# Linear attention with a gated feed-forward block on one core: the last rows' stacks spread over two stages, the bias loaded into the accumulators

## The chip, the cores and the metric

The kernel runs on one core of a Trainium2 chip. The metric is the device time of one execution in microseconds; lower is better. The core's engines work side by side, each through its own list of instructions: TensorE (PE) multiplies matrices, VectorE (DVE), ScalarE (ACT) and GpSimd (POOL) work on tiles, and the Sync queue (SP) issues most of the transfers (DMAs). A core has 16 DMA engines for them.

## The reference

With x of 2048 rows by 576 columns, 32 heads of 18 columns and a hidden width of 4608:

```
xn = layernorm(x)
q, k, v = split(xn @ wqkv)                       # per head
phi(t) = where(t > 0, t + 1, exp(t)) + 1e-6
kv = sum_s phi(k)[s] v[s]^T ; z = sum_s phi(k)[s]
o  = (phi(q) kv) / (phi(q) z + 1e-6)
s  = o @ wo
g  = silu(gelu(xn @ w1 + b1) @ w2 + b2)
out = x + s * g
```

All is float32. The matrix products are made from operands split into a high and a low part (hi: a rounded copy; lo: the difference), three products of parts for one.

## The kernel before

**Three stages.** The kernel is one long list, written out by hand. Every product runs on TensorE; around it a table `plans` holds what the other engines do and after which step of TensorE's work it is issued (`add(step, function)` puts an entry, `at_step(step)` issues the entries of a step in the order in which they were put). `in_order` makes the order of the list binding on each engine.

*Keys and values* (pairs p = 0 to 7, steps p * 14 + k, lines 542 to 775): a pair is two tiles of 128 rows of x. They are loaded, normalized, transposed and split; stored for later (`x_store`); a projection `Proj` (line 362) makes the keys of both tiles from seven products in the order 1, 6, 7, 5, 2, 4, 3, then `Plain` makes the values, and `do_state` (step 3) adds the pair before to the state. Beside it, operands for the second feed-forward matrix are prepared: `w2_sum` adds blocks, `w2_hi` (line 530) copies the hi part on ScalarE, `w2_lo` subtracts on VectorE and stores the result to memory. `W2_SPLITS` says at which (pair, step of hi, step of lo).

*Queries* (iterations r = 0 to 9, steps (8 + r) * 14 + k, lines 793 to 1218): `Proj` again makes queries of two tiles, phi and the denominators follow on ScalarE, VectorE and GpSimd, `transpose_p` transposes the quotients, and `Attend` of two iterations before multiplies them by the state folded with wo.

*Feed-forward* (two halves of x's rows with nine chunks of hidden columns each, 28 steps a chunk, lines 1613 to 1728): `Up` makes hidden columns with seven products (steps 0 to 13), gelu and the hi/lo split `HOps` follow, and `product` multiplies by W2 into four accumulators C11, C12, C21, C22 and a helper U1 of the tile `macc` (steps 14 to 27). At a chunk's steps 12, 13, 15 and 17 of a half's first chunk `set_bias` (line 1257) fills the accumulators with b2. Later chunks' weight operands are loaded on the Sync queue at given steps (`W1Loaded` makes its tiles and loads; `W2_NEXT` for W2).

**The wait that the restart of bank e can bring.** A projection has four accumulators in PSUM: a, b, z, e. Product 5 goes into e, VectorE adds it to a running term (line 399, through the helper at line 386), and product 3, the last, goes on adding into the same bank:

```
elif i == 5:
    self.mm(E, 5, (1, 1))
    add1(b[:, HD:], E, self.u2)
...
elif i == 3:
    self.mm(E, 3, (1, 2), first=False)
    add1(a[:, HD:], E, self.u1)
```

**The stacks of the last rows.** 576 rows are four tiles of 128 and 64 rows left over. For these `Rest` (line 912) makes stacks, seven in all: two of x's, five of W1's. A stack is loaded (256 KB); `hi(g)` and `lo(g)` split three (g = 0) or four (g = 1) of its column blocks on ScalarE and VectorE; `sums` makes on VectorE, between the two groups, four sums in place that group 1 is made of; `store(g)` writes hi and lo, each twice, to memory from where the feed-forward stage loads them. The load lies in iteration r = 1 to 6 (stack 0 before the iterations) at step 1; hi, lo of group 0 and the sums at step 2 of the next iteration (step 5 for r = 1), group 1 three steps later, stores two steps after each.

**Pools.** The groups' tiles come from `w1r`, tag `stw`, two buffers that are taken in turn. The same tag serves the operands of `w2_hi`, the temporaries of `wkq.sums` and the raw W1 tiles. The stack's raw columns come from `stage`, six buffers, as the x tiles do.

**The bias.** `load_bias` (line 1250) loads b2, the same row in all 128 partitions, into a tile with the tag `w2t6`, which is also the tag of `load_sum(7)` (line 1331), issued at step 5 of chunks 0 to 7. It runs before the first chunk and at step 2 of the second half's first chunk. `set_bias` copies from the tile.

## Time and profile before

| | |
|---|---|
| median of three runs | 1129.63 us (1128.88 to 1129.68) |
| the profiled execution | 1128.63 us, span 1126.9 us |
| granted TensorE clock, mean | 0.993 |
| busy: PE, PE weight loads | 97%, 90% |
| busy: DVE, ACT, POOL | 73%, 46%, 40% |
| moved by the DMA engines | 295.02 MB, mean 262 GB/s |

A page of the profile gives busy times and the chain of work that ended last; the other views answer for a stretch, a line or a tile. In a row of the waits stand engine, tile and line of the instruction that waited, what released it, and total, number and longest of the waits in us. In a timeline row stand start, duration, engine, line, operation, what is written from what, and in square brackets the idle time ahead of it with the releaser. A row of the windows has the busy time of PE, weight loads, DVE, ACT and POOL in a stretch with the number of instructions, then the granted clock (1.00 is full), the mean share in which the DMA engines were busy, and GB/s. Where TensorE's clock is granted at less than 1.00, part of the stretch ran slower. Pairs 2 to 6 of the first stage begin at 48.9, 65.85, 83.08, 100.31 and 117.55 us, the queries at about 150 us, the feed-forward stage at about 308 us and its second half at about 713 us.

### The profile page before, as it was taken

How to read it: one execution, taken by the hardware profiler on the slowest of the kernel's cores; microseconds unless marked ns; L12 is line 12 of the kernel's file. 1: busy time of each engine (PE TensorE's matmuls, PEld its weight loads, DVE VectorE, ACT ScalarE, POOL GpSimd, SP SyncE). 2: the span in 40 equal slices, each digit the busy share in tenths (PEclk: the TensorE clock that was granted, in tenths of full speed). 3: DMA queues.
4: the chain of work that ended last, by engine and by line, in shares of the span. 5: the costliest groups of instructions: out<-in, count | busy, mean ns of one | idle time of the engine just before them, and what ended most of it. 6: DMA issues, size and time to landing. Idle time of an engine off the chain costs nothing.

```text
span 1126.9 us, 18961 instructions
## 1 busy us (share of the span) xinstructions
PE 1096.0 (97%) x6888; PEld 1011.6 (90%) x6888; DVE 822.2 (73%) x1288; ACT 517.4 (46%) x945; POOL 456.0 (40%) x417
## 2 busy tenths in 40 slices
PE   8999997898999999999999999999999999999998
PEld 8999997888989989889899899898998998989988
DVE  6777577778578878888888888675575664765866
ACT  7776454454564543544545435444233242332342
POOL 6853522454552644534525434224133232241310
PEclk9999998999999999999999999999999999999999
DMA  5997839898998796886977969998767667767243
GB/s 199 320 287 263 287 90 316 303 358 301 318 380 271 269 359 202 294 314 220 341 249 248 360 170 351 381 356 305 221 221 226 211 222 229 222 221 236 86 151 116
DMA packets 115771, 295.02 MB, mean 262 GB/s; under 512 B 12189, under 2 KB 31133, under 8 KB 113631
## 3 DMA queue, kind: packets, MB, share of 16 engines
q1 hardware_dynamic: 110207, 282.61, 71.2%
q0 software_dynamic: 4896, 10.03, 5.3%
q8 instruction: 54, 0.88, 0.3%
q10 hardware_dynamic: 576, 1.18, 0.3%
q14 instruction: 38, 0.31, 0.1%
HBM read 180.39 MB, written 108.66 MB: 256 GB/s over the span
## 4 chain that ended last, share of the span: by engine, by line
PE 69%; DMA 1%; DVE 1%; ACT 1%; issue 1%; DVEq 0%; ACTq 0%
PE pm L1418 34%; PE zy L1279 10%; PE a L1279 10%; PE e L1279 10%; PE b L1279 5%; PE pd L1533 2%; DMA op<-w 1%; DMA op_b<-wb 1%; DVE macc L1526 0%; ACT macc L1527 0%; DVE h_l L1000 0%; DVE b L1305 0%; ACT g L1287 0%; ACT L1287 0%; DVE xs L1477 0%
## 5 line engine op out<-in xcount | busy, mean ns | idle before, releaser
L997 ACT CAST h_h<-g 128x512 fp32r<-128x512 f32 x204 | 120.1, 621 | 135.9 <-PE pm L1418 134.9
L1000 DVE TENSOR_TENSOR h_l<-g,h_h 128x512 fp32r<-128x512 f32 x204 | 160.2, 785 | 3.8 <-ACT h_h L997 3.8
L1426 DVE TENSOR_TENSOR macc<-macc,pm 128x576 f32<-128x576 f32 x136 | 102.1, 751 | 39.3 <-PE pm L1418 39.3
L1279 PE MATMUL a<-xH,wa 128*128 128x512 f32 x288 | 101.4, 393 | 0.0
L1428 DVE TENSOR_TENSOR macc<-pm,macc 128x576 f32<-128x576 f32 x98 | 74.2, 757 | 21.9 <-PE pm L1418 20.2
L1386 POOL TENSOR_TENSOR mid<-g 128x512 f32<-128x512 f32 x34 | 45.4, 1334 | 100.2 <-ACT g L1287 100.2
L1287 ACT ACTIVATE g<-b,b1c 128x512 f32<-128x512 f32 x36 | 24.8, 688 | 131.7 <-DVE b L1305 131.7
L1296 ACT COPY mid<-a 128x512 f32<-128x512 f32 x36 | 21.2, 588 | 94.1 <-PE a L1279 94.1
L1279 PEld LDWEIGHTS a<-xH,wa 128*128 128x128 f32 x288 | 54.0, 188 | 11.3
L1380 POOL TENSOR_TENSOR g<-g 128x512 f32<-128x512 f32 x34 | 50.6, 1490 | 24.1 <-DVE h_l L1000 22.5
L1299 DVE TENSOR_TENSOR mid<-b,mid 128x512 f32<-128x512 f32 x36 | 24.7, 685 | 44.6 <-PE b L1279 42.7
L1279 PE MATMUL a<-xL,wa 128*128 128x512 f32 x144 | 56.2, 390 | 0.0
L1383 POOL TENSOR_TENSOR g<-g 128x512 f32<-128x512 f32 x34 | 50.8, 1493 | 11.3 <-DVE h_l L1000 9.0
L1504 POOL TENSOR_TENSOR fin1l<-fin1h,fin1l 128x288 f32<-128x288 f32 x8 | 6.5, 807 | 120.5 <-PE pm L1418 44.5
L1279 PE MATMUL e<-xSH,wb 128*128 128x512 f32 x144 | 50.4, 391 | 0.8 <-DVE b L1305 0.8
L1279 PE MATMUL zy<-xSH,w 128*128 128x512 f32 x144 | 50.9, 394 | 0.0
L1279 PE MATMUL zy<-xH,w 128*128 128x512 f32 x144 | 50.8, 394 | 0.0
L1279 PE MATMUL b<-xSH,w 128*128 128x512 f32 x144 | 50.5, 391 | 0.0
L1279 PE MATMUL e<-xSH,w 128*128 128x512 f32 x144 | 50.4, 390 | 0.0
L1024 POOL TENSOR_TENSOR mid<-w1raw 128x256 f32<-128x256 f32 x17 | 14.9, 877 | 85.4 <-DMA w1raw<-w 51.0
L1377 POOL TENSOR_TENSOR g<-g 128x512 f32<-128x512 f32 x34 | 47.6, 1399 | 2.7
L1000 DVE TENSOR_TENSOR h_l<-mid,h_h 128x512 fp32r<-128x512 f32 x34 | 42.3, 1245 | 7.3 <-ACT h_h L997 7.3
(965 smaller groups left out, 3674.0 us busy)
## 6 DMA issues: line engine op xcount, KB each, us to landing
op<-w SPq DMA_DIRECT2D x72, 256.0 KB, 5.3
w<-op SPq DMA_DIRECT2D x72, 256.0 KB, 3.6
we<-we_dram SPq DMA_DIRECT2D x36, 448.0 KB, 4.8
w2raw<-w SPq DMA_DIRECT2D x10, 1152.0 KB, 10.1
op<-w2o SPq DMA_DIRECT2D x19, 576.0 KB, 6.1
w1raw<-w SPq DMA_DIRECT2D x18, 512.0 KB, 6.4
op_a<-wa SPq DMA_DIRECT2D x18, 512.0 KB, 4.5
wa<-op_a SPq DMA_DIRECT2D x18, 512.0 KB, 4.3
```

The costliest lines, as they stand in the source:

```text
L997: nc.scalar.copy(pair[0], src)
L1000: eng.tensor_tensor(pair[1], src, pair[0].bitcast(F32), op=SUB)
L1279: nc.tensor.matmul(ps.rearrange("p (c j) -> p c j", c=4), st, mv, start=first and n == 0, stop=n == len(seq) - 1, skip_group_check=True,)
L1287: nc.scalar.activation(g, ps, AF.Gelu_apprx_tanh, bias=b1c[:, f : f + 1])
L1299: tt(u1_sb, B, m1_sb, op=ADD)
L1377: tt(src[5, pr], A(1, 1), A(1, 0), op=SUB)
L1380: tt(src[6, pr], src[5, pr], A(0, 0), op=ADD)
L1383: tt(src[3, pr], src[6, pr], A(0, 1), op=SUB)
L1386: tt(src[7, pr], A(0, 0), A(1, 0), op=SUB)
L1418: nc.tensor.matmul(ps[:, q, :HD], hs[p][st][:, cs], m[:, p, :], start=(n == 0 and i not in CHAIN), stop=(n == len(seq) - 1), skip_group_ch ...
L1426: nc.vector.tensor_tensor(dst, dst, src, op=SUB)
L1428: nc.vector.tensor_tensor(dst, src, dst, op=ADD)
```

## The change

`Rest` moves ahead of the first stage, keeps a tile for each group, and its `sums` takes the engine as an argument. A table places all seven stacks: three (x's first, W1's first and second) beside keys and values, the other four in the queries, mostly one group an iteration. An entry gives the load as (pair or iteration + 8, step), the step of group 0's lo, place and engine of the sums, and the step of group 1's lo; hi comes one step before lo, the store one step after (two in one case).

```
+    REST_PLAN = {
+        (0, True): ((2, 12), (3, 2), (3, 4, GP), (4, 2)),
+        (0, False): ((4, 0), (5, 2), (5, 13, DV), (6, 2)),
+        (1, False): ((4, 7), (5, 2), (5, 13, DV), (6, 2)),
+        (2, False): ((8, 9), (9, 12), (9, 12, DV), (10, 6)),
+        (3, False): ((9, 9), (10, 6), (10, 11, DV), (11, 6)),
+        (4, False): ((11, 1), (12, 6), (12, 9, DV), (13, 6)),
+        (1, True): ((13, 1), (14, 6), (14, 9, DV), (15, 6)),
+    }
+
+    def plan_rests():
+        for key, (load, first, (p, k, eng), second) in REST_PLAN.items():
+            add(load[0] * NSP + load[1], lambda key=key: rests.update({key: Rest(*key)}))
+            for g, (q, at) in enumerate((first, second)):
+                step = q * NSP + at
+                add(step - 1, lambda key=key, g=g: rests[key].hi(g))
+                add(step, lambda key=key, g=g: rests[key].lo(g))
+                add(step + (2 if step == 9 * NSP + 12 else 1), lambda key=key, g=g: rests[key].store(g))
+            add(p * NSP + k, lambda key=key, eng=eng: rests[key].sums(eng))
+
+    plan_rests()
     for p in range(1, NPAIR):
         plan_pair(p)
...
-    rests = {0: Rest(0, True)}
-    RESTS = ((0, True), (0, False), (1, False), (2, False), (3, False), (4, False), (1, True))
...
-        if 0 < r < NPAIR - 1:
-            i, of_x = RESTS[r]
-            add(base + 1, lambda r=r, i=i, of_x=of_x: rests.update({r: Rest(i, of_x)}))
-        if 1 <= r < NPAIR:
-            at = base + (5 if r == 1 else 2)
-            for g, k in ((0, 0), (1, 3)):
-                add(at + k, lambda r=r, g=g: rests[r - 1].hi(g))
-                add(at + k, lambda r=r, g=g: rests[r - 1].lo(g))
-                add(at + k + 2, lambda r=r, g=g: rests[r - 1].store(g))
-            add(at, lambda r=r: rests[r - 1].sums())
```

One split of a W2 operand moves from steps 4 and 6 of pair 5 to steps 7 and 9:

```
-        (2, 4, 6), (2, 9, 12), (3, 4, 6), (3, 9, 12), (4, 4, 6), (4, 9, 12), (5, 4, 6), (6, 7, 9), (7, 1, 3),
+        (2, 4, 6), (2, 9, 12), (3, 4, 6), (3, 9, 12), (4, 4, 6), (4, 9, 12), (5, 7, 9), (6, 7, 9), (7, 1, 3),
```

The bias is loaded straight into the first of four row blocks of C11 and of C22, and `set_bias` copies from there to the other three blocks and to C21 and C12. In the second half the load moves from step 2 to step 8, behind the W2 load that stands at that step; two loads of W2 operands come eight steps earlier:

```
+    BIAS = (C11, C22)
+
     def load_bias():
-        b2b = fr.tile([P, 2, HD], F32, tag="w2t6", name="b2b", bufs=1)
-        nc.sync.dma_start(
-            b2b.rearrange("p a b -> p (a b)"), bass.AP(tensor=b2.tensor, offset=b2.offset, ap=[[0, P], [1, D]])
-        )
-        tails["b2"] = b2b
+        for h, m in enumerate(BIAS):
+            src = bass.AP(tensor=b2.tensor, offset=b2.offset + h * HD, ap=[[0, P], [1, HD]])
+            nc.sync.dma_start(macc[:, 0, m, :], src)
 
     def set_bias(s):
-        h = int(s in (C12, C22))
-        nc.scalar.copy(macc[:, :, s, :], tails["b2"][:, h : h + 1].to_broadcast([P, QH, HD]))
+        m = BIAS[s in (C12, C22)]
+        at = slice(s == m, QH)
+        dst = macc[:, at, s, :]
+        nc.scalar.copy(dst, macc[:, 0:1, m, :].to_broadcast(list(dst.shape)))
...
-    W2_SUMS_FIRST = {4: 4, 5: 6, 6: 18}
+    W2_SUMS_FIRST = {4: 4, 5: 6, 6: 10}
...
-                add(base + 2, load_bias)
+                add(base + 8, load_bias)
             for at, m in zip((12, 13, 15, 17), (C11, C22, C21, C12)):
                 add(base + at, set_bias, m)
...
-                    add(base + at + (19 if swap and i == 6 else 11 * swap), lambda i=i, n=step + 1: w2t[n].load(i))
+                    add(base + at + 11 * swap, lambda i=i, n=step + 1: w2t[n].load(i))
```

An assertion at the end of the plan, which makes no instruction, is new as well.

More of the change, by code (lines that the diff above doesn't have):

```diff
@@ L313, in x_lo, with __init__, hi, lo @@
         tt(r, src[64:, 4], r.bitcast(F32), op=SUB)
+    class Rest:
+        def __init__(self, i, of_x=False):
+            self.i, self.of_x, self.t = i, of_x, {}
+            self.s = stage(4 * P, f"rs{i}{of_x}").rearrange("p (k c) -> p k c", k=4)
+            nc.sync.dma_start(self.s, xr_dram[i] if of_x else w1e[i].rearrange("p (k c) -> p k c", k=4))
+        def hi(self, g):
+            n = (3, 4)[g]
+            t = w1r.tile([P, 2, 4, P], F32R, tag="stw", name=f"re{self.i}{self.of_x}{g}")
+            self.t[g] = t = t[:, :, :n]
+            nc.scalar.copy(t[:, 0], self.s[:, :n])
+        def lo(self, g):
+            t, n = self.t[g], (3, 4)[g]
+            nc.vector.tensor_tensor(t[:, 1], self.s[:, :n], t[:, 0].bitcast(F32), op=SUB)
+        def store(self, g):
+            t, at = self.t.pop(g), slice(3 * g, (3, 7)[g])
+            n = t.shape[2] * P
+            for j in range(2):
+                v = t[:, j].bitcast(F32).rearrange("p i j -> p (i j)")[:, None].to_broadcast([P, 2, n])
+                if self.of_x:
+                    dst = xe_dram[self.i].rearrange("(a b r) c i j -> b (r c) a (i j)", a=2, b=2)[j]
+                else:
+                    dst = we_dram[self.i].rearrange("(b a r) c i j -> b (r c) a (i j)", a=2, b=2)[j]
+                nc.sync.dma_start(dst[:, :, at.start * P : at.stop * P], v)
+        def sums(self, eng):
+            a, b, c, d = (self.s[:, k] for k in range(4))
+            tt = eng.tensor_tensor
+            if self.of_x:
+                tt(d, a, d, op=SUB), tt(c, c, d, op=SUB), tt(a, c, a, op=ADD), tt(b, b, c, op=SUB)
+            else:
+                tt(a, d, a, op=SUB), tt(d, c, d, op=SUB), tt(c, c, a, op=SUB), tt(b, b, c, op=SUB)
     def x_rest(p, s):
@@ L910, in p_lo @@
         nc.vector.tensor_tensor(th[64:, 4, :], p3[64:, 4, :], th[64:, 4, :].bitcast(F32), op=SUB)
-    class Rest:
-        def __init__(self, i, of_x=False):
-            self.i, self.of_x = i, of_x
-            self.s = stage(4 * P, f"rs{i}{of_x}").rearrange("p (k c) -> p k c", k=4)
-            nc.sync.dma_start(self.s, xr_dram[i] if of_x else w1e[i].rearrange("p (k c) -> p k c", k=4))
-        def hi(self, g):
-            n = (3, 4)[g]
-            t = w1r.tile([P, 2, 4, P], F32R, tag="stw", name=f"re{self.i}{self.of_x}{g}")
-            self.t = t[:, :, :n]
-            nc.scalar.copy(self.t[:, 0], self.s[:, :n])
-        def lo(self, g):
-            t, n = self.t, (3, 4)[g]
-            nc.vector.tensor_tensor(t[:, 1], self.s[:, :n], t[:, 0].bitcast(F32), op=SUB)
-        def store(self, g):
-            t, at = self.t, slice(3 * g, (3, 7)[g])
-            n = t.shape[2] * P
-            for j in range(2):
-                v = t[:, j].bitcast(F32).rearrange("p i j -> p (i j)")[:, None].to_broadcast([P, 2, n])
-                if self.of_x:
-                    dst = xe_dram[self.i].rearrange("(a b r) c i j -> b (r c) a (i j)", a=2, b=2)[j]
-                else:
-                    dst = we_dram[self.i].rearrange("(b a r) c i j -> b (r c) a (i j)", a=2, b=2)[j]
-                nc.sync.dma_start(dst[:, :, at.start * P : at.stop * P], v)
-        def sums(self):
-            a, b, c, d = (self.s[:, k] for k in range(4))
-            tt = nc.vector.tensor_tensor
-            if self.of_x:
-                tt(d, a, d, op=SUB), tt(c, c, d, op=SUB), tt(a, c, a, op=ADD), tt(b, b, c, op=SUB)
-            else:
-                tt(a, d, a, op=SUB), tt(d, c, d, op=SUB), tt(c, c, a, op=SUB), tt(b, b, c, op=SUB)
     class Attend:
@@ L1088, in linear_attention_gated_ffn @@
     EL1 = nc.vector
+    kept = []
     w1t, w2_raw0 = {}, []
@@ L1728, in linear_attention_gated_ffn @@
                 at_step(base + 14 + 2 * k + q2 // 2)
+    assert not plans, sorted(plans)
     ws = [w2t[step].ops["p", f] for f in range(CF)]
```

2 lines of the change are left out of this document (1 added, 1 removed).

## The prediction

> **What bounds the kernel now.** Read first: busy time and waits of TensorE. It is busy for 97% of the span, and its waits lie almost all in one place.
>
> ```profile
> PE 1096.0 (97%) x6888; PEld 1011.6 (90%) x6888; DVE 822.2 (73%) x1288; ACT 517.4 (46%) x945; POOL 456.0 (40%) x417
> PE e L378 <- DVE rt L386: 10.1, 3, 5.6
> PE e L378 <- DVE scr L386: 7.1, 3, 2.7
> PE a L378 <- ACT scr L390: 1.7, 1, 1.7
> ```
>
> The columns of the waits are total us, times, longest. Six waits of 17.2 us together stand ahead of a matmul into bank e (line 378), the last product of a query projection. It adds to what the fourth product left there, so VectorE must have read the bank first (the additions of line 386). With the 1.7 us for the Scalar copy of line 390, 18.9 us of TensorE's idle time are in the queries. Next, the stretches from one restart of bank e to the next: columns length, busy time by engine (instructions), granted clock, transfer share, GB/s.
>
> ```profile
> 186.47:205.64 19.17, 16.94 (x117) 16.71 (x117) 14.28 (x29) 8.08 (x18) 6.40 (x5) 0.91 1.00 360
> 205.64:224.82 19.18, 16.95 (x116) 16.72 (x116) 15.67 (x26) 8.87 (x19) 9.58 (x6) 0.91 0.80 279
> 224.82:243.19 18.37, 15.70 (x116) 15.23 (x117) 15.42 (x26) 9.46 (x19) 9.06 (x6) 1.00 0.98 361
> 243.19:262.37 19.18, 16.95 (x116) 16.72 (x116) 14.49 (x26) 8.75 (x19) 9.57 (x6) 0.91 0.98 348
> 262.37:279.99 17.62, 15.43 (x117) 15.21 (x117) 14.32 (x26) 9.37 (x19) 9.61 (x6) 1.00 0.80 298
> ```
>
> The same matmuls take 16.94 to 16.95 us in the three iterations at a granted clock of 0.91, and 15.70 and 15.43 us in the two at 1.00. A slow stretch so costs 16.95 - 15.57 = 1.4 us; three cost 4.2. A stretch's length less TensorE's busy time is the wait at its end: the slow ones come behind the longest wait (5.6) and behind 2.23 and 2.67 us, while two other waits of 2.23 us were followed by a full clock. What the waits cost in all is 18.9 + 4.2 = 23.1 us. Now the timeline of VectorE and TensorE at one wait (start, duration):
>
> ```profile
> 221.49 0.35 DVE L878 RECIPROCAL den<-den 128x32 f32<-128x32 f32 x1
> 221.76 0.49 DVE L927 TENSOR_TENSOR re2False<-rs2False,re2False 128x384 fp32r<-128x384 f32 x1
> 222.29 2.11 DVE L946 TENSOR_TENSOR rs2False<-rs2False 128x128 f32<-128x128 f32 x4
> 224.31 0.45 DVE L386 SCALAR_TENSOR_TENSOR rt<-e,scr 128x288 f32<-128x288 f32 x1
> 226.26 1.63 DVE L927 TENSOR_TENSOR re2False<-rs2False,re2False 128x512 fp32r<-128x512 f32 x1
> 222.17 0.29 PE L378 MATMUL z<-wkq_rh,xH 128*128 128x288 f32 x1
> 222.30 0.29 PE L378 MATMUL z<-wkq_rl,xH 128*128 128x288 f32 x1
> 224.82 0.40 PE L378 MATMUL e<-wkq_h,xSH 128*128 128x288 f32 x1 [2.23 <-DVE rt L386]
> ```
>
> TensorE has issued its last z matmul at 222.30 and, at 0.13 us apart, would go on at 222.43. VectorE is then in a stack's first subtraction (0.49) and its four sums (2.11, three of them 0.29 and one drawn out), which the plan puts ahead of the addition that frees bank e. The second subtraction (1.63) follows and delays only the next addition.
>
> **The queries without those steps.** From the third iteration to the last, the hi copy is at step 5, the subtraction at step 6, behind the last addition, and the sums at steps 9 to 12. Ahead of the critical addition stands the reciprocal, ending at 221.84; with 0.45 for the addition bank e is free at 222.3, before 222.43. So the wait goes; what is late next is z's own addition, with 0.1 us to spare, and for the five later iterations I leave 0.5 us in all. The steps that stay delay the exponentials by at most one subtraction (1.63), as the second one does now. A tile of the two-buffer pool is then taken three times an iteration and not four; a W2 operand still has to wait for a stack's stores as before.
>
> In iteration 2 the wait is longer, for another reason:
>
> ```profile
> 173.75 1.14 DVE L944 TENSOR_TENSOR rs0True<-rs0True 128x128 f32<-128x128 f32 x4
> 175.48 0.78 ACT L465 ACTIVATE e<-scr,c 128x576 f32<-128x576 f32 x1 [2.13 <-DVE scr L386]
> 176.83 0.60 ACT L923 CAST re0True<-rs0True 128x512 fp32r<-128x512 f32 x1
> 177.34 0.77 ACT L471 ACTIVATE scr<-scr,c 128x576 f32<-128x576 f32 x1
> 178.44 0.40 PE L378 MATMUL a<-wkq_h,xH 128*128 128x288 f32 x1 [1.66 <-ACT scr L390]
> 183.52 0.51 ACT L923 CAST re0False<-rs0False 128x384 fp32r<-128x384 f32 x1 [3.30 <-DMA xe_dram<-re0True]
> ```
>
> The hi copy at 183.52 waited 3.30 us for the stores of the stack before, and the addition stands behind it. The new plan has one group ahead of this projection (step 12 of iteration 1): copy, subtraction, sums. Without the old sums the exponentials start about 1.6 us sooner (1.14 + 0.49), near 173.9; two of them (0.78), line 471 (0.77) and the new group's copy (0.51) end near 176.7, its subtraction (0.49) and sums (1.14) near 178.4. Three additions (0.45 each) and the p splits, for which I put 1 us by the copies of that tile's size (0.78), bring bank e free near 180.8. TensorE could have gone on at 176.8 (178.44 less 1.66); it waits 0.3 us for the copy of line 390, has 16 matmuls of 0.13, and wants bank e near 179.2. That leaves about 2.0 of the 7.3 us lost here (1.7 + 5.6; bounds 0 and 7.3). Term A: 23.1 - 2.0 - 0.5 = **20.6 us saved** (bounds 15.3 and 23.1).
>
> [...]
>
> **Keys and values with three stacks.** Each stack brings a load (256 KB), two ScalarE copies (0.51, 0.60), two subtractions (0.49 and at most 1.63), four sums (1.14 to 2.11; the x stack's go to GpSimd in pair 3, which is busy for 7.90 of 17.23 us there) and four stores. The stage as it is, pairs 3 to 6, and the rows around pair 5's restart of bank e:
>
> ```profile
> 65.85:83.08 17.23, 17.23 (x138) 17.23 (x138) 12.90 (x30) 11.34 (x23) 7.90 (x11) 1.00 0.95 276
> 83.08:100.31 17.23, 17.23 (x138) 17.23 (x138) 12.94 (x30) 11.35 (x23) 7.27 (x10) 1.00 0.90 313
> 100.31:117.55 17.24, 17.24 (x138) 17.24 (x138) 12.26 (x29) 10.86 (x23) 8.90 (x16) 1.00 0.72 223
> 117.55:134.00 16.45, 16.45 (x131) 16.45 (x131) 9.18 (x19) 8.62 (x19) 5.35 (x5) 1.00 0.83 302
> 104.05 0.46 DVE L386 SCALAR_TENSOR_TENSOR k<-e,mu 128x288 f32<-128x288 f32 x1
> 107.26 0.29 PE L378 MATMUL e<-wkq_h,xSH 128*128 128x288 f32 x1
> 100.60 1.23 ACT L279 ACTIVATE xn<-x,mv 128x576 f32<-128x576 f32 x2
> 102.52 1.04 SPq L540 DMA_DIRECT2D op<-w2o  x1
> DMA to landing us min/median/max: 5.9/5.9/5.9
> ```
>
> TensorE is never idle; VectorE and ScalarE are idle for over 4 us of each pair. In pair 5 the addition ends at 104.51 and bank e is wanted at 107.26: the state's matmuls and a transposition lie between. This is the cover, 2.75 us. Two subtractions at step 2 (1.0 us) fit; each us beyond costs one. But both copies stand at step 1 of pair 5, and each takes a tile of the pool with two buffers. By the order of allocation the second takes the buffer of pair 4's second W2 operand. Its store was issued at 102.52, since the Sync queue holds it behind the x stores, and stores of this kind landed 5.9 us after issue here: at 108.4. ScalarE is ready at 101.8, so it stands 6.6 us, with the x splits of step 3 behind it; VectorE stands at the subtraction, with the addition behind. 108.4 + 0.51 + 0.49 + 0.46 and 0.15 of hand-over give 110.0: TensorE waits 2.8 us, and after 2.67 us it lost the clock above, so 1.4 more. Term B: **4.2 us lost**. Bounds: 0 (an earlier store hides it) and 7.3 (landing after 9.0 us, as the slowest stack store below). In pair 6 the same two copies come, but the operand before them is split earlier in its pair and the cover there is larger; I take nothing. The extra sums at step 13 (twice 1.14) fill VectorE's idle time. Loads of x run two pairs ahead, so stores ahead of them on the Sync queue cost nothing.
>
> ```profile
> we_dram<-re0False SPq DMA_DIRECT2D x2, 512.0 KB, 5.7
> we_dram<-re1False SPq DMA_DIRECT2D x2, 384.0 KB, 9.0
> ```
>
> A stack stores 2 x 512 + 2 x 384 KB; with its load three stacks are 6.1 MB.
>
> **The bias.** In the first half nothing is lost: the Sync queue waited 9.7 us for the old bias tile, and no engine waited for what was behind. The new load is 20 us ahead of its use, as the old was. So 0 there, also for the W2 loads brought forward (bounds 0 and -0.5, the TensorE waits of that chunk). In the second half the load moves from step 2 to step 8, its first use stays at step 12, and ScalarE works in the written order:
>
> ```profile
> SPq L1334 <- ACT macc L1259: 9.7, 1, 9.7
> 735.84 0.32 SPq L1357 DMA_DIRECT2D w__8368<-op  x1
> DMA to landing us min/median/max: 7.0/7.2/9.5
> 736.10 1.14 ACT L1259 COPY macc<-b2b 128x1152 f32<-128x1152 f32 x1
> 737.14 0.62 ACT L997 CAST h_h<-g 128x512 fp32r<-128x512 f32 x1
> 739.21 0.53 PE L1418 MATMUL pm<-w__8258,h_h 128*128 128x288 f32 x2
> ```
>
> Step 8 of the Sync queue is the W2 load issued at 735.84: it has stood behind seven weight loads of step 7. The bias load goes out behind it, at 736.2. Loads issued between 700 and 760 landed after 7.0 to 9.5 us (the row without a line number). So the bias is there at 743.4, and ScalarE, ready at 736.1, stands 7.3 us. Behind it is the hi copy that now starts at 737.14, an operand of the second product, which TensorE began at 739.21 and whose second half it wants 0.4 us later. Bias (3 of 4 rows, 0.86), copy 0.62 and the lo part's lag of 0.4: 743.4 + 0.86 + 0.62 + 0.4 - 739.6 = 5.7 us of waiting, and 1.4 for the clock. Term C: **7.1 us lost**. Bounds: 0 (a landing within 1.5 us) and 9.4 (9.5). The bias copies are shorter by 0.29 twice; they are off the path.
>
> **Sum.** -20.6 + 4.2 + 7.1 = -9.3 us. The profiled execution took 1128.63 us (span 1126.9 and 1.7 around it), 1.0 under the median of 1129.63. I forecast 1129.63 - 9.3 = **1120.3 us**; one term at a time at a bound, short of B or C being nothing, gives 1117.8 (A), 1122.6 (C), 1123.4 (B) and 1125.6 (A).
>
> **Rivals.** (1) The bias comes in time, because the transfers have run empty there or the Sync queue reaches step 8 sooner: -16.4, 1113.2 us (1109 if B is hidden as well). For it: other small loads are not shown to wait. Against: the landing times. (2) The stack's buffer is free in time, C stays: -13.5, 1116.1 us. For it: the share falls to 0.72 in pair 5. Against: the 102.52. (3) The queries stay late: subtractions and sums put elsewhere leave about 1 us at each of five restarts and the three slow stretches; -20.6 becomes -11.4, and with B and C -0.1: 1129.5 us. For it: VectorE's margin is 0.1 us. Against: its idle time later in the iteration. (4) Slower: keys and values become paced by transfers. The 6.1 MB take 20.5 us at the 300 GB/s of pairs 3 to 6. Their shares leave 0.05 + 0.10 + 0.28 + 0.17 of a pair, 10.2 us; if these are times when nothing could be issued, all 20.5 us lengthen the stage, in place of B: -20.6 + 20.5 + 7.1 = +7.0, 1136.6 us. It decides from 15.8 us unhidden on. For it: shares of 0.90 to 0.95. Against: TensorE waited for no transfer in these pairs.
>
> **How the numbers follow.** Forecast 0.46, (1) 0.24, (2) 0.12, (3) 0.11, (4) 0.07. The range 1110 to 1127 takes in the forecast with its bounds, (1) and (2) and the faster half of (3); it leaves out (4), half of (3) and the ends of the bounds, some 0.17. A measurement of this kernel tells about 0.2% from no change, 2.26 us. Faster: 0.46 + 0.24 + 0.12 + 0.04 = 0.86; within: 0.07 of (3); slower: (4), 0.07.
>
> **What would show it.** Right: the waits of bank e for line 386 in the queries sum to under 4 us, and the iterations run at 15.4 to 15.7 us with the clock at 1.00; one new wait of bank e in pair 5 (near 107 us), with ScalarE held by a store of a W2 operand; ScalarE held at the bias copy in the second half for about 7 us and TensorE waiting on a product's lo or hi part there. Wrong: restarts still a us late or more (A), no wait in pair 5 (B), no wait at the bias (C), or TensorE idle in several pairs of the first stage (4).

## The result, and the profile after

The changed kernel takes 1138.45 us (median of four runs, 1137.64 to 1140.56) against 1129.26 us before (four runs, 1128.85 to 1129.68). The ratio is 1.0084, 95% interval 1.0067 to 1.0102: slower by 9.2 us, where 1120.3 us and a gain of 9.3 were forecast. The profiled execution has a span of 1135.9 us, 9.0 more than before.

First the span by stages, from the start of pair 3 to the first query iteration, from there to the feed-forward stage, and to the end; the changed kernel, then the kernel before, over the same work (columns as in the prediction: length, busy time of PE, weight loads, DVE, ACT and POOL, clock, transfer share, GB/s).

```profile
64.60:160.00 95.40, 89.42 (x667) 88.74 (x666) 62.72 (x134) 53.09 (x102) 41.16 (x52) 0.95 0.90 301
160.00:308.40 148.40, 138.94 (x979) 133.93 (x978) 115.47 (x192) 72.01 (x150) 67.66 (x50) 0.95 0.73 259
308.40:1135.90 827.50, 815.13 (x4813) 739.49 (x4812) 601.72 (x854) 342.20 (x606) 297.31 (x264) 0.99 0.75 254
```

```profile
64.60:149.20 84.60, 84.60 (x668) 84.60 (x667) 56.86 (x120) 51.33 (x97) 40.76 (x48) 1.00 0.83 269
149.20:306.90 157.70, 138.33 (x978) 133.02 (x978) 117.43 (x210) 75.19 (x154) 69.09 (x49) 0.96 0.80 281
306.90:1126.90 820.00, 813.37 (x4813) 736.84 (x4812) 601.62 (x854) 342.58 (x606) 300.17 (x264) 1.00 0.76 257
```

Keys and values lost 95.4 - 84.6 = 10.8 us, the queries gained 157.7 - 148.4 = 9.3, and the rest lost 827.5 - 820.0 = 7.5. The forecast for the three was 4.2 lost, 20.6 gained and 7.1 lost. Before the change TensorE had not a gap in the first of these stages and its clock was 1.00 throughout; now it is busy for 89.42 of 95.40 us and the clock is 0.95. TensorE's waits in the changed kernel:

```profile
PE pm L1430 <- DVE macc L1442: 5.7, 1, 5.7
PE e L414 <- DVE k L422: 5.6, 2, 3.2
PE ptp L956 <- DVE th L968: 3.8, 2, 1.9
PE a L414 <- ACT scr L426: 3.1, 1, 3.1
PE z L414 <- DVE scr L432: 1.2, 1, 1.2
```

The waits for `rt` and `scr` at bank e, 17.2 us before, are gone but for one of 0.2 us. In their place stand one wait in the second half, two at bank e among the keys and values, and four in the queries.

**Pair 3**, a place to which the prediction gave nothing. The Sync queue's, ScalarE's, VectorE's and TensorE's rows (start, duration; idle time ahead in brackets):

```profile
67.24 0.41 SPq L320 DMA_DIRECT2D rs0True<-xr_dram  x1
73.85 0.51 ACT L326 CAST re0True<-rs0True 128x384 fp32r<-128x384 f32 x1 [6.51 <-issue]
74.39 0.56 DVE L330 TENSOR_TENSOR re0True<-rs0True,re0True 128x384 fp32r<-128x384 f32 x1 [4.95 <-ACT re0True L326]
74.87 0.45 DVE L422 SCALAR_TENSOR_TENSOR k<-e,mu 128x288 f32<-128x288 f32 x1
75.38 0.40 PE L414 MATMUL e<-wkq_h,xSH 128*128 128x288 f32 x1 [2.44 <-DVE k L422]
```

The stack's own load goes out at 67.24. ScalarE reaches the hi copy 0.1 us later (73.85 - 6.51 = 67.34) and stands for 6.51 us; the profile names no releaser, and the load of the copy's input is what it had to wait for (stores_away below keeps this wait without the stores). VectorE stands at the subtraction, and the addition that frees bank e is the instruction behind it. The load had been planned at step 12 of the pair before, three steps ahead of the copy; on the queue it came behind that pair's last x stores, issued at 65.92 and 66.34, at the first of which the queue had stood 4.7 us for GpSimd's part of the split (line 386).

**Pair 5**, the place that was forecast:

```profile
106.17 2.01 SPq L576 DMA_DIRECT2D op<-w2o  x1
113.30 0.51 ACT L326 CAST re1False<-rs1False 128x384 fp32r<-128x384 f32 x1 [6.67 <-issue]
114.83 0.61 PE L414 MATMUL e<-wkq_h,xSH 128*128 128x288 f32 x1 [3.19 <-DVE k L422]
```

By the order in which the two buffers are taken, the copy at 113.30 takes the one that the W2 operand stored at 106.17 leaves, 7.1 us after the issue; ScalarE stood for 6.67 us. Here too the profile names no releaser. The load of the copy's own input was issued at 99.00; in stores_away the same load, issued at 97.87, was there by 108.62 at the latest, so the store is the likelier one, but no run separates the two.

**The queries.** The stretches from one iteration's first product to the next: iterations 1 and 2 together, then 3 to 5.

```profile
176.30:206.90 30.60, 26.28 (x179) 25.51 (x177) 22.80 (x47) 14.87 (x31) 9.82 (x9) 0.89 0.78 258
206.90:222.80 15.90, 15.65 (x118) 15.18 (x117) 14.66 (x22) 8.82 (x20) 10.84 (x8) 1.00 0.89 326
222.80:240.10 17.30, 15.39 (x120) 15.19 (x118) 16.02 (x25) 8.61 (x19) 9.12 (x7) 1.00 0.86 312
240.10:256.80 16.70, 16.70 (x119) 16.70 (x117) 12.46 (x21) 7.82 (x16) 8.53 (x6) 0.90 0.93 338
```

Iteration 3 runs nearly as forecast: 15.65 us busy, the clock at 1.00. Iteration 4, and 6 like it, ends in a wait, and the one behind it runs at 0.90: the same matmuls take 16.70 instead of 15.39 us. At the end of iteration 4:

```profile
235.07 3.46 DVE L349 TENSOR_TENSOR rs4False<-rs4False 128x128 f32<-128x128 f32 x4
238.46 0.68 DVE L967 TENSOR_TENSOR tl<-ptp,th 128x512 fp32r<-128x512 f32 x1
239.15 0.29 DVE L968 TENSOR_TENSOR th<-ptp,th 64x128 fp32r<-64x128 f32 x1
239.59 0.80 PE L956 MATMUL ptp<-ident,pbuf 128*128 128x128 f32 x5 [1.91 <-DVE th L968]
```

Four sums of a stack, drawn out to 3.46 us, stand ahead of the lo part of p's transposition, and only that frees the bank for the next transposition. The sums had been put at step 9, the step of this lo part, and the table of stacks is put in first. In iteration 2 the group that iteration 1 takes is late:

```profile
180.09 1.35 SPq L320 DMA_DIRECT2D rs2False<-w1e  x1
190.36 0.51 ACT L326 CAST re2False<-rs2False 128x384 fp32r<-128x384 f32 x1 [2.81 <-DMA rs2False<-w1e]
190.78 0.39 ACT L426 COPY scr<-a 128x288 f32<-128x288 f32 x1
191.22 0.40 PE L414 MATMUL a<-wkq_h,xH 128*128 128x288 f32 x1 [3.11 <-ACT scr L426]
```

The load, planned at step 9 of iteration 0, goes out at 180.09, when the fold's shifts are through the queue; the hi copy waits 2.81 us for it, and the copy of bank a, which TensorE wants, is next on ScalarE. **The second half:**

```profile
736.76 1.02 SPq L1265 DMA_DIRECT2D macc<-b  x2
743.12 0.91 ACT L1271 COPY macc<-macc 128x864 f32<-128x864 f32 x1 [5.81 <-DMA macc<-b]
744.58 0.69 DVE L1022 TENSOR_TENSOR h_l<-g,h_h 128x512 fp32r<-128x512 f32 x1 [6.76 <-ACT h_h L1019]
746.00 0.85 PE L1430 MATMUL pm<-w__8258,h_h 128*128 128x288 f32 x2 [5.73 <-DVE macc L1442]
```

The bias is issued at 736.76, used at 743.12 after 5.81 us of waiting, and behind it come the product's operand (its hi copy at 743.94, its lo part at 744.58) and the copy that frees its bank: term C as it was worked out, 5.73 us of waiting against 5.7.

### The profile page after: what moved, and what is told of

Its sections match the earlier page's. It is cut to its first block, busy times and chain, and to the rows that moved or that the text cites. A ratio compares the mean times of both kernels' runs of the same rounds, so it can differ in the third digit from the quotient of the medians.

```text
span 1135.9 us, 18977 instructions
## 1 busy us (share of the span) xinstructions
PE 1102.8 (97%) x6888; PEld 1018.9 (90%) x6888; DVE 826.5 (73%) x1284; ACT 515.7 (45%) x945; POOL 452.5 (40%) x421
## 4 chain that ended last, share of the span: by engine, by line
PE 79%; DMA 7%; DVE 6%; ACT 3%; issue 3%; POOL 1%; SPq 1%; DVEq 0%; POOLq 0%; ACTq 0%
PE pm L1430 33%; PE zy L1291 10%; PE a L1291 9%; PE e L1291 9%; PE b L1291 5%; PE ps_s L989 4%; PE pd L1545 2%; PE e L414 1%; PE pl L470 1%; PE z L414 1%; DMA wa<-op_a 1%; DMA rs2False<-w1e 1%; PE a L414 1%; DMA op<-w2o 1%; DMA op<-w 1%
## 5 line engine op out<-in xcount | busy, mean ns | idle before, releaser
L1440 DVE TENSOR_TENSOR macc<-pm,macc 128x576 f32<-128x576 f32 x98 | 74.2, 757 | 24.9 <-PE pm L1430 23.5
L1395 POOL TENSOR_TENSOR g<-g 128x512 f32<-128x512 f32 x34 | 51.3, 1508 | 12.5 <-DVE h_l L1022 10.4
L676 POOL TENSOR_TENSOR zacc<-zacc,k 128x576 f32<-128x576 f32 x16 | 25.6, 1602 | 53.2 <-ACT k L507 52.6
```

Source lines behind the costliest of these rows:

```text
L1395: tt(src[3, pr], src[6, pr], A(0, 1), op=SUB)
L1440: nc.vector.tensor_tensor(dst, src, dst, op=ADD)
```

## The experiments

Thirteen kernels were run, each beside the kernel before on the same chip. Ratios are to the kernel before, with their 95% intervals; the changed kernel is at 1.0084. The table has, in us from the timeline of TensorE, the length of pairs 3 to 7 and iteration 0, of iterations 1 and 2 together, and of iterations 3 to 6, from first product to first product.

| kernel | ratio | pairs 3, 4, 5, 6, 7 | it. 0 | 1 and 2 | 3, 4, 5, 6 |
|---|---|---|---|---|---|
| before | 1 | 17.2, 17.2, 17.2, 16.7, 16.2 | 15.8 | 32.6 | 19.2, 17.7, 19.9, 17.7 |
| changed | 1.0084 | 21.5, 17.2, 23.3, 16.7, 16.8 | 16.3 | 30.5 | 15.9, 17.3, 16.7, 17.3 |
| old_bias | 1.0005 (0.9994 to 1.0016) | 21.5, 17.2, 23.5, 16.7, 16.4 | 17.0 | 30.1 | 16.1, 17.4, 16.6, 17.5 |
| groups_later | 1.0088 (1.0071 to 1.0106) | 18.0, 25.6, 17.2, 17.5, 18.0 | 16.3 | 29.9 | 16.0, 17.3, 15.2, 19.0 |
| sums_later | 1.0056 (1.0043 to 1.0069) | 21.4, 17.2, 23.3, 16.7, 17.5 | 16.4 | 29.2 | 16.1, 15.2, 15.9, 16.9 |
| load_earlier | 1.0085 (1.0063 to 1.0107) | 21.5, 17.2, 23.7, 16.7, 17.3 | 16.3 | 29.9 | 16.0, 17.3, 16.7, 17.3 |
| stores_away | 1.0050 (1.0033 to 1.0067) | 21.5, 17.2, 17.2, 16.7, 16.2 | 15.8 | 31.0 | 16.0, 19.2, 15.2, 20.5 |
| later_stores_away | 1.0032 (1.0017 to 1.0046) | 17.9, 17.2, 17.2, 16.7, 16.2 | 15.8 | 29.9 | 16.0, 20.4, 16.5, 19.4 |
| bias_earlier | 1.0003 (0.9993 to 1.0012) | 21.5, 17.2, 22.4, 16.8, 16.8 | 16.9 | 29.6 | 16.1, 17.3, 16.7, 17.4 |
| one_step_later | 0.9976 (0.9966 to 0.9986) | 17.2, 17.2, 17.2, 16.7, 16.2 | 15.8 | 31.7 | 16.8, 17.9, 19.3, 18.8 |
| two_repairs | 0.9974 (0.9964 to 0.9983) | 21.4, 17.2, 23.5, 16.7, 17.5 | 16.5 | 30.3 | 16.0, 15.2, 15.6, 17.2 |
| four_repairs | 0.9968 (0.9952 to 0.9983) | 17.2, 18.9, 17.5, 16.7, 16.9 | 23.6 | 29.5 | 16.0, 15.2, 15.6, 17.2 |
| five_repairs | 0.9937 (0.9921 to 0.9954) | 17.2, 19.7, 17.5, 16.7, 16.2 | 22.3 | 23.6 | 17.7, 16.7, 19.2, 15.2 |
| three_early | 0.9909 (0.9897 to 0.9922) | 17.2, 17.2, 17.9, 16.8, 17.3 | 19.2 | 23.6 | 17.4, 16.7, 19.3, 16.1 |
| two_early | 0.9887 (0.9872 to 0.9902) | 17.2, 17.2, 17.9, 16.8, 17.0 | 16.3 | 23.6 | 17.4, 16.7, 19.5, 17.0 |

The theory to test was that the loss is a handful of waits, each on one landing or one written order, with a slow stretch behind each. Its rival was that a resource is full: the transfers in the keys and values, VectorE in the queries.

**The bias undone** (old_bias: `load_bias` and `set_bias`, step 2 and the old steps of the W2 loads, as before the change).

> The changed kernel with the bias as it was before (a tile of its own, loaded at step 2; the W2 loads at their old steps). Theory: in the second half ScalarE stands at the bias copy until the load has landed, and the products behind it wait 5.7 us and run their first 5 us at a granted clock of 0.50 to 0.85; all of that goes: -7.5 us, 1131 us, and no TensorE wait for macc. Rival (the loads of that half are late whichever comes first, since the queue carries seven weight loads at that place): the wait moves to a weight load, and the time falls by 2 us at most, to 1136.5 or more.

1.0005: with 0.9994 to 1.0016 no difference from before is left, 0.79% of 1130 us or 8.9 us less than the changed kernel, where 7.5 were expected (the two intervals allow about 2 us either way). The wait for `macc` is gone and none came for a weight load. The bias part cost the whole of its term, and what the rest of the change gave and took nearly cancels.

**The bias load three steps sooner** (bias_earlier).

```
-                add(base + 8, load_bias)
+                add(base + 5, load_bias)
```

> The changed kernel with the bias load of the second half at step 5 instead of 8. Theory (ScalarE stands until the load has landed 6.3 us after its issue): the load is issued near 731.5 instead of 736.8, lands near 738.5, ScalarE waits about 1.5 us instead of 5.8 and TensorE 1 us instead of 5.7, with a shorter slow stretch: -5 to -6 us against the changed kernel, 1133 us. Rival (the load cannot go out before the stores of the first half's sums have landed, and holds the weight loads behind it on the queue): the wait of TensorE moves to a weight load, and the time stays at 1137 us or more.

1.0003, 9.2 us less than the changed kernel where 5 to 6 were expected. The two rows are the load's issue and the first bias copy:

```profile
727.53 6.01 SPq L1265 DMA_DIRECT2D macc<-b  x2
737.48 0.90 ACT L1271 COPY macc<-macc 128x864 f32<-128x864 f32 x1
```

The rival's mechanism is there: the Sync queue stands at this load for 6.01 us, 4.8 of them for the store of the first half's sums (`c_dram<-macc`) from the same tile. But the seven weight loads behind it come early enough nonetheless, and ScalarE copies without a gap. So the load into the accumulators costs nothing at step 5, and 5.7 us and a slow stretch at step 8.

**Two groups behind the addition** (groups_later).

```
-        (0, True): ((2, 12), (3, 2), (3, 4, GP), (4, 2)),
+        (0, True): ((2, 12), (3, 6), (3, 8, GP), (4, 2)),
-        (1, False): ((4, 7), (5, 2), (5, 13, DV), (6, 2)),
+        (1, False): ((4, 7), (5, 6), (5, 13, DV), (6, 2)),
```

> The changed kernel with two of the six early groups four steps later in their pair (pair 3's first from step 2 to step 6, its sums from step 4 to step 8; the second of pair 5's from step 2 to step 6), behind the addition that frees bank e; the same loads, stores and bytes. Theory (one landing each, and the engines' written order): no wait of bank e in pairs 3 and 5, both pairs back at 17.2 us: -4.3 and -6.1, together -10.4 us, 1128 us. Rival (the transfers of three more stacks pace the stage): the bytes are the same, so the two pairs or those behind them stay long, and the time falls by less than 3 us, to 1135.5 or more.

1.0088, and the theory's 10.4 us did not come, though both places were repaired: pair 3 went from 21.5 to 18.0 and pair 5 from 23.3 to 17.2 us. Pair 4 took 8.4 us of it back, 25.6 us, pairs 6 and 7 another 2.0:

```profile
85.89 0.78 SPq L576 DMA_DIRECT2D op<-w2o  x1
98.92 0.67 ACT L569 CAST w2o<-w2r 128x576 fp32r<-128x576 f32 x1 [8.21 <-DMA op<-w2o]
100.42 1.33 PE L289 MATMUL pt<-ident,xn 128*128 128x128 f32 x5 [5.46 <-ACT xn L279]
```

A W2 operand's copy waited 8.21 us for the store of the operand two takes back in the ring, issued at 85.89 and landed only 13 us later; the normalization behind it held the transposition. The ring is the same there as in the changed kernel, where this copy waited 2.09 us, at no cost to TensorE, for a store that had landed about 8 us after its issue: there the stack's first stores went out at 74.39, 11.7 us ahead of pair 4, here at 78.56, 4.3 us ahead. So the loss moved, as the rival had it, and two readings were left: a queue that is too full for three more stacks, or only a ring of two buffers in which a long landing is passed on.

**The stacks' stores taken out of the stage** (stores_away with the groups in place, later_stores_away with the edit above). Both leave out the early stacks' stores and store other stacks twice, so three stacks in memory hold another stack's rows.

```
+            key = self.i, self.of_x
+            if key in AWAY:
+                return
+            for i in [self.i] + [k[0] for k, v in AWAY.items() if v == key]:
+                self.store_to(i, t, at)
```

> The changed kernel without the stores of its three early stacks (5.4 MB) in the keys and values; in their place the stacks of iterations 4 to 6 are stored twice, so that three stacks in DRAM hold another stack's rows. Copies, subtractions, sums and loads stay where they are. Read from the start of pair 3 to the start of the query iterations (68.4 us for pairs 3 to 6 before the change, 78.7 after it). If the written order alone makes the loss: pair 3 still waits for the stack's load (4.3 us) and pair 5 for the store of a W2 operand (at least 3 of its 6 us): pairs 3 to 6 take 75.5 us or more. If the transfers pace the stage: 19.0 MB instead of 24.4 MB are moved as before the change, and pairs 3 to 6 take 70 us or less. The queries get the bytes instead, so the whole time says less: 1128 to 1136 us.

> The same without these stores, with pair 3's first group and one of pair 5's four steps later (the edit that moved the loss from pairs 3 and 5 into pair 4). If the transfers were what held pair 4: pairs 3 to 6 take 68.4 to 69.5 us, TensorE waits for nothing there. If it is the written order (a W2 operand's copy behind a group that came four steps later): pair 4 stays long by 4 us or more and the four pairs take 73 us or more.

Pairs 3 to 6 took 72.6 us in the first, between the two forecasts: pair 3 kept its 4.3 us, which settles that it is the load and not the stores, and pair 5 lost nothing. In the second the four pairs took 69.0 us, inside the forecast for transfers that hold the stage (68.4 to 69.5). I had taken this for a test of the bytes, and it is not a clean one:

```profile
108.62 0.51 ACT L328 CAST re1False<-rs1False 128x384 fp32r<-128x384 f32 x1 [2.20 <-DVE re0False L332]
```

Without its store a group's tile is free after its subtraction, and the second copy of pair 5 took that tile (released by `re0False` at line 332) and not the W2 operand's. Bytes and buffer had gone together, so these runs do not say which of them made the 6.1 us.

**The sums behind p's lo part** (sums_later: two of the table's `(…, 9, DV)` become step 10).

```
-        (4, False): ((11, 1), (12, 6), (12, 9, DV), (13, 6)),
-        (1, True): ((13, 1), (14, 6), (14, 9, DV), (15, 6)),
+        (4, False): ((11, 1), (12, 6), (12, 10, DV), (13, 6)),
+        (1, True): ((13, 1), (14, 6), (14, 10, DV), (15, 6)),
```

> The changed kernel with the sums of two stacks one step later (iterations 4 and 6, step 9 to step 10), behind the lo part of the query transposition. Theory: VectorE's four drawn-out sums (3.46 us) stood ahead of the lo part that frees the transposition's bank; the two TensorE waits of 1.91 us go, and with them the slow stretch behind each (1.3 us): -6.4 us, 1132 us. Rival (VectorE is simply full in these iterations, 16.0 of 17.3 us): the sums delay the next addition of bank e or the split behind it by as much, waits come up there, and the time falls by 2 us at most, to 1136.5 or more.

1.0056, 3.2 us less than the changed kernel where 6.4 were expected. Both waits at the transposition are gone, iterations 4 to 6 take 15.2, 15.9 and 16.9 us, and from the start of the queries to the feed-forward stage pass 142.5 us instead of 148.4. Not all of these 5.9 us are the edit's: iterations 4 to 6 gained 3.3 and what comes behind them 1.4, together 4.7, while 1.3 lie in iterations 1 and 2, which it doesn't touch and which took 29.2 to 31.0 us in the kernels that leave them as they are. And 3.1 were given back at the bias, where the wait of TensorE grew from 5.7 to 8.8 us. VectorE was not too full; with the bias repaired too (two_repairs) both gains hold.

> The changed kernel with two of the edits at once: the bias load of the second half at step 5, and the sums of iterations 4 and 6 one step later. If the places are independent: the 7 to 8 us of the bias and the 5.6 us that the sums gave by the first product of the first half, -13 us against the changed kernel, 1126 us, 0.996 of before. If what is gained at the front is given back at the bias (with the sums alone the wait there grew from 5.7 to 8.8 us): the load at step 5 comes late again, TensorE waits 3 us or more for macc, and 1129 us or more.

0.9974, which is 12.4 us less than the changed kernel against 13 expected, and there is no wait for `macc`.

**The load ahead of the fold's shifts** (load_earlier).

```
-        (2, False): ((8, 9), (9, 12), (9, 12, DV), (10, 6)),
+        (2, False): (None, (9, 12), (9, 12, DV), (10, 6)),
...
-                0: [lambda: phi_max(a, e_bufs[0]), lambda: phi_max(b, e_bufs[1])],
+                0: [lambda: rests.update({(2, False): Rest(2)}), lambda: phi_max(a, e_bufs[0]), lambda: phi_max(b, e_bufs[1])],
```

> The changed kernel with the load of the stack that iteration 1 splits (w1e 2) issued inside the fold of wo, ahead of the fold's shifts on the Sync queue, some 7 us sooner. Theory: the hi copy no longer waits for the landing, TensorE's waits of 3.1 and 1.2 us in iteration 2 go and the slow stretch behind them (14.5 us of work at a granted clock of 0.78, 3.2 us) with them, and the 2 us of bank e that were forecast for this place come up instead: -5.5 us, 1133 us. Rival (iteration 2 is late by VectorE's and ScalarE's own work, exponentials and splits, as it was before the change): the same loss at bank e, the time falls by 1.5 us at most, to 1137 or more.

1.0085: nothing. The load was in time, ScalarE's copy came at 188.46, TensorE's wait at bank a fell from 3.11 to 0.19 us, and the next wait took its place:

```profile
188.99 1.48 DVE L330 TENSOR_TENSOR re2False<-rs2False,re2False 128x384 fp32r<-128x384 f32 x1 [0.58 <-ACT re2False L326]
190.50 2.36 DVE L349 TENSOR_TENSOR rs2False<-rs2False 128x128 f32<-128x128 f32 x4
193.33 0.46 DVE L432 TENSOR_TENSOR scr<-z,scr 128x288 f32<-128x288 f32 x1
193.84 0.61 PE L414 MATMUL z<-wkq_h,xH 128*128 128x288 f32 x1 [3.21 <-DVE scr L432]
```

The group's subtraction and sums, 3.8 us on VectorE, stand ahead of the two additions of iteration 2 (lines 429 and 432); TensorE waits at bank z for the second. The rival was right that this iteration is late by VectorE's work; which work is told by the run below that moves the group (five_repairs).

**The kernel before with its stacks one step later** (one_step_later), the test of term A by itself: all seven stacks stay in the queries.

```
-            at = base + (5 if r == 1 else 2)
+            at = base + (5 if r == 1 else 3)
```

> The kernel before with one edit: from iteration 2 on both groups and the sums of a stack come one step later (3 and 6 instead of 2 and 5), so that VectorE's subtraction and sums stand behind the addition that frees bank e and not ahead of it. All seven stacks stay in the queries, the same bytes at nearly the same places. Theory (TensorE's 17 us at bank e are this written order and nothing else): five waits of 2.2 to 2.8 us go, most of the 7 us in iteration 2 stay or halve, and the slow stretches go: -10 to -17 us against before, 1113 to 1120 us. Rival (VectorE is too full, the work only moves): the exponentials and the next p split come late by the same 2.1 us, waits of 2 us come up at the transposition of p or at bank a, and the time falls by less than 3 us, to 1127 or more.

0.9976, 2.7 us and not 10 to 17. The waits of bank e are gone, and others stand in their place:

```profile
PE ptp L898 <- DVE th L910: 6.1, 5, 1.5
PE z L378 <- ACT s L975: 3.2, 2, 1.8
222.35 4.40 DVE L946 TENSOR_TENSOR rs2False<-rs2False 128x128 f32<-128x128 f32 x4
```

Here the rival is right: with two groups and their sums in every iteration, right behind the critical addition, the sums (4.40 us) delay the last additions and with them exponentials, denominators and p's lo part. So the order at bank e had hidden a second limit. That work can be moved, but not by one step: sums_later and five_repairs gain with the sums at step 10, behind p's lo part.

**The early stacks spread anew** (four_repairs is two_repairs with the three lines below; five_repairs moves in addition the stack that iteration 1 split).

```
+        (0, True): ((3, 3), (4, 3), (4, 4, GP), (5, 3)),
+        (0, False): ((4, 7), (5, 11), (5, 13, DV), (6, 3)),
+        (1, False): ((6, 7), (7, 8), (7, 10, DV), (7, 12)),
...
+        (2, False): ((8, 9), (10, 6), (10, 10, DV), (11, 3)),
+        (3, False): ((10, 9), (11, 6), (11, 10, DV), (12, 3)),
```

> The two edits, and the three early stacks spread anew over the keys and values: one group at a time, four of the six behind the addition that frees bank e (step 3), pair 3 without any, loads nearly a pair ahead, the last stack in pair 7 (groups at steps 8 and 12), where the transfer share falls. All bytes stay in the stage, over pairs 4 to 7 instead of 3 to 6. Theory (pair 3 lost 4.3 us to the landing of a load right ahead of its use, pair 5 6.1 us to a store that landed late in a queue filled with the stacks' stores): both go or nearly, the stage from pair 3 to the queries takes 85 to 87 us (84.6 before the change, 95.4 after it), 1117 us, 0.988 of before. Rival (the transfers of the stage leave no room for 6 MB, wherever they are put): the loss moves to pairs 4 to 7, 92 us or more for the stage, 1124 us or more.

> The same, with the stack that iteration 1 split (w1e 2) moved to iterations 2 and 3 and the one behind it to 3 and 4, each group at step 3 or 6 and the sums at step 10. Theory: in iteration 2 the wait of bank a (3.1 to 3.6 us, ScalarE's copy behind the hi copy) and of bank z or e behind VectorE's subtraction and sums go, iterations 1 and 2 take 27 to 28 us instead of 30.6; iterations 3 and 4 get two groups each and lose 1 us: -2 to -3 us against the run before, 1114 us. Rival (one step later over all iterations gave only 2 us, because VectorE was too full with two groups and drawn-out sums): iterations 3 and 4 lose 2 us each, and it is no faster than the run before.

In four_repairs pairs 3 to 7 took 87.2 us, at the end of the theory's 85 to 87, and yet the time was 0.9968 and not 0.988: iteration 0 took 23.6 us, because the hi copy in pair 7 waited for its stack's sums ahead of the last v copy (TensorE waited 4.7 us for v). In five_repairs iterations 1 and 2 fell from 29.5 to 23.6 us, about twice what was expected: the group is now split behind the additions of iteration 2's projection, and TensorE is busy for 23.49 of 23.60 us at full clock. Iterations 3, 4 and 5 paid 1.6, 1.6 and 3.6 us with the groups as they now lie, iteration 6 gained 2.0; the whole was 0.9937.

**What is left: full queues or the order?** Both runs put the first stack's groups to step 11 of pair 4 and step 6 of pair 5. three_early keeps all three stacks beside keys and values, as below; in two_early the entry of the third is `((12, 9), (13, 6), (13, 10, DV), (14, 3))`, iterations 5 and 6 (and x's second stack and W1's last are shifted by some steps to make room).

```
+        (0, True): ((3, 9), (4, 11), (5, 3, GP), (5, 6)),
+        (0, False): ((4, 7), (5, 12), (5, 13, DV), (6, 3)),
+        (1, False): ((6, 7), (7, 8), (7, 8, DV), (7, 12)),
```

> The five repairs with the same first early stack (step 11 of pair 4, step 6 of pair 5) and the third stack left in pair 7, its sums two steps sooner (step 8), so that the hi copy behind them no longer waits for them ahead of the last v copy. Theory: pair 4's 2.5 us go as in the other run, of iteration 0's 6 us about 3: -5 us, 1118 us. If VectorE's splits of the query weights stand in pair 7 behind the earlier sums, the v copy stays as late: -2.5 us, 1120.5 us.

> The kernel of the five repairs with only two early stacks, the third (w1e 1) in iterations 5 and 6, so that the queries hold five stacks, and the first early stack's groups late in pair 4 (step 11) and in pair 5 (step 6) instead of step 3 of both. Theory: pair 4 lost 2.5 us because the group at step 3 took a buffer in the ring of two and so put a W2 operand's copy behind a store issued only some 10 us sooner (ScalarE waited 5.0 us), and the start of the queries lost 6 us because a hi copy of pair 7 stood ahead of the last v copy (TensorE waited 4.6 us). Both places are empty now: pairs 3 to 7 take 84.6 to 85.6 us as before the change, iteration 0 16.2 us instead of 22.3, iterations 5 and 6 lose 1 us: -7 us against the five repairs, 1116 us, 0.987 of before. Rival (the transfers or VectorE are full wherever a stack goes): what is gained there is lost in iterations 3 to 7, the time falls by less than 2 us.

three_early is at 0.9909, about 1120 us, between its two forecasts; two_early at 0.9887, 1117.3 us against 1130.4 before on that chip, where 1116 was expected. The stage in three_early, pairs 3 to 7:

```profile
65.50:151.90 86.40, 85.14 (x667) 84.60 (x666) 59.59 (x128) 52.34 (x101) 41.34 (x52) 1.00 0.90 304
```

The stage takes 86.4 us: 1.8 more than before the change, while the changed kernel lost 10.8 in the same five pairs. The rate alone proves nothing: it is 304 GB/s at a share of 0.90, as the changed kernel had 301 and 0.90, and 86.4 us at 304 are 26.3 MB where 95.4 at 301 are 28.7. The third stack's last stores fall into iteration 0. Over pairs 3 to 7 and iteration 0 together both kernels move 29.2 MB, the kernel before 23.1; three_early, the changed kernel and the kernel before:

```profile
65.55:171.15 105.60, 101.42 (x766) 97.67 (x764) 73.70 (x152) 61.98 (x120) 45.08 (x54) 1.00 0.82 276
64.60:176.34 111.74, 105.51 (x766) 102.06 (x764) 74.36 (x152) 61.77 (x120) 44.61 (x54) 0.95 0.78 261
64.62:165.00 100.38, 100.38 (x765) 97.76 (x764) 67.43 (x138) 59.10 (x114) 43.48 (x50) 1.00 0.71 230
```

The same bytes cost 105.6 - 100.4 = 5.2 us in one order and 11.4 in the other, and 2.9 of the 5.2 are one wait of TensorE for v in iteration 0, behind the stack's work in pair 7. Nor were the changed kernel's 301 GB/s all that the stage can move: two_early has 311 at a share of 0.93 in pairs 3 to 7. So it is the order and not the bytes that makes at least 6.1 of the 11.4 us; whether transfers make any of the 2.3 us that are left is not shown. A landing took 5.9 us after its issue before the change, 7.1 in pair 5 and 13 in groups_later, and that costs only where a copy is next in the ring or next behind a load. two_early is the fastest kernel of the case; what it still waits for is the ring again (ScalarE's W2 copies wait for a stack's stores, and the copies behind them free the bank that z takes):

```profile
PE z L414 <- ACT s L997: 6.6, 4, 2.5
226.09 0.67 ACT L569 CAST w2o<-w2r 128x576 fp32r<-128x576 f32 x1 [2.07 <-DMA we_dram<-re3False]
```

## Why the prediction was wrong

**The sum was -20.6 + 4.2 + 7.1; measured are -9.3, +10.8 and +7.5.**

*Term C held* in its mechanism and its wait: the place on the queue, the landing, the hi copy behind the bias copy and the wait (5.73 us against 5.7). old_bias and bias_earlier show it from both sides. Only the slow stretch was too small: from 746 to 752 us the clock was 0.50, which is 3.0 us and not 1.4. That the stage lost 7.5 us, so near to 7.1, is partly luck.

*Term A was cut in half, and the step that failed is "So the wait goes; what is late next is z's own addition".* The wait at bank e did go; what was late next was another. Only the addition's own neighbours had been followed, not the step to which the sums moved. There they stand ahead of p's lo part: twice 1.91 us and two slow stretches of 16.70 - 15.39 = 1.3, together 6.4 us; sums_later, without these waits, gained 4.7 us there. (The slow stretch is not certain behind such a wait: in the kernel before the clock was 1.00 behind two of 2.23 us, and in groups_later, where iteration 4 took the same 17.3 us, iteration 5 took 15.2 us and not 16.7.) The other 4.6 us are iteration 2, for which a gain of 7.3 - 2.0 + 1.4 = 6.7 was in the sum and 32.6 - 30.5 = 2.1 came. The working for iteration 2 put the new group's copy near 176.2 by ScalarE's work and left out the group's own load, which this queue issues behind the fold's shifts. load_earlier shows that the load alone was not the end of it: the subtraction and the sums ahead of the additions cost as much, and only with the group behind them (five_repairs) does the stretch fall to 23.6 us. 9.3 + 6.4 + 4.6 = 20.3 of the 20.6.

*Term B had the right mechanism in pair 5 (as far as a profile without a releaser there can tell), with too small a size, and missed pair 3.* In pair 5 the wait was 3.19 us against 2.8, with a landing 7.1 instead of 5.9 us after the store's issue; the slow stretch behind it cost 23.3 - 17.2 - 3.19 = 2.9 instead of 1.4. Pair 3 has no term in the sum, and the step that put it at nothing is "Loads of x run two pairs ahead, so stores ahead of them on the Sync queue cost nothing": it speaks of x's loads and leaves out the stack's own, which is planned three steps ahead of its copy, waited on the Sync queue behind the x stores and cost 4.2 us (2.44 of waiting, 1.8 of slow clock). 4.2 and 6.1 us and 0.6 in pair 7 are the 10.8 to within 0.1. (Pair 6, for which the prediction took nothing, lost nothing.)

*The rivals.* The slower one (transfers pace the stage) named a time near the measured one, 1136.6 us, but not its reason, and that is luck: three_early moves the same 29.2 MB by the end of iteration 0 in 6.1 us less. Rival (3), the queries staying late, met the size (-11.4 against -9.3), but not the place: it was p's transposition and iteration 2, not the restarts of bank e.

*The clock.* The forecast took a slow stretch to cost 1.4 us, by the stretches of the kernel before. In the changed kernel the clock is at half behind the gap of 2.44 us in pair 3, from 76.3 to 79.7 us, and behind the one of 1.91 us in iteration 4, from 240.1 to 243.6 us (behind others of that length it stays full, as the last section has it). Stretches of 2 us from the end of each gap:

```profile
75.38:77.38 2.00, 2.00 (x11) 2.00 (x12) 1.92 (x7) 1.84 (x4) 1.05 (x3) 0.73 1.01 374
77.38:79.38 2.00, 2.00 (x11) 2.00 (x10) 2.00 (x7) 1.15 (x2) 0.00 (x0) 0.50 0.91 286
239.59:241.59 2.00, 2.00 (x11) 2.00 (x12) 1.31 (x2) 0.15 (x1) 0.00 (x0) 0.64 0.29 116
241.59:243.59 2.00, 2.00 (x11) 2.00 (x10) 0.21 (x1) 0.99 (x2) 0.00 (x0) 0.51 0.95 251
```

So gaps of this length can cost clock, as the forecast took it; its 1.4 us a stretch was too little behind the longer ones (2.9 us behind 3.19 us in pair 5, 3.0 behind 5.73 us in the second half).

## What to carry to other kernels

When a step is moved, write down for the new place what stands behind it on its engine, and follow each operand's own load back through its queue to the instructions that hold that queue; the waits that cost here were the moved work's, not the old work's. A gap that is closed brings stores, landings and takes of buffers behind it closer together (in groups_later the stack's first stores went out 4.3 us ahead of pair 4 and not 11.7), so a repair is judged by the whole stage and by what is late next: groups_later gave most of what it gained back in pair 4, sums_later 3.1 of 5.9 us at the bias. When a full resource is suspected, move the bytes and keep their sum (three_early), and compare over a stretch that holds them all; leaving them out can free a buffer as well.

## What the runs showed of the hardware

**The clock after a gap.** These are TensorE's gaps of 1 us and more between 45 and 800 us in the profiles of the kernel before and of the changed kernel. With those of 3.11, 3.19, 5.63 and 5.73 us went a clock of 0.50 for 6.8 us each (192.35 to 199.18, 113.84 to 120.67, 183.01 to 189.84 and 745.31 to 752.14; the last three began before the gap had ended). Behind those of 1.13 us (328.93) and 1.66 us (178.44) the clock stayed at 1.00; one of 1.16 us (193.75) lies inside the first of these stretches. Between them it went both ways: 0.50 for 3.4 us behind 1.91 us (239.59 and 273.60), 2.23 (205.64), 2.44 (75.38) and 2.67 us (243.19), 1.00 behind 2.19 us (279.99) and 2.23 us (224.82 and 262.37). In iteration 0 of three_early, with its wait for v, TensorE was idle for 2.9 of 19.3 us and the clock was 1.00. The gap of 3.19 us cost 2.9 us more behind it. What decides between the two in the middle was not tried.

**VectorE beside GpSimd.** Four sums of 128x128 took 1.14 us in the prediction's row at 173.75, with nothing on GpSimd from 173 to 176 us, and 1.27 us in iteration 2 of the changed kernel (191.50 to 192.77, where GpSimd begins at 192.52), but 3.46 us in the row at 235.07, while GpSimd was in two multiplications:

```profile
235.44 1.53 POOL L926 TENSOR_TENSOR e<-rt,zb 128x576 f32<-128x576 f32 x1 [0.90 <-ACT rt L507]
236.93 1.46 POOL L926 TENSOR_TENSOR scr<-rt,zb 128x576 f32<-128x576 f32 x1
```

In one_step_later four took 4.40 us (222.35), and GpSimd was in three instructions from 222.05 to 226.28. No run here took GpSimd's work away from beside them, so what draws them out is not shown.
